# Row maxima folded into PSUM and the last stage's mask made by ScalarE, in a fused attention and mixture-of-experts kernel

## The chip, the cores and the metric

The kernel runs on one core of one Trainium2 chip. The metric is the device time of one execution in microseconds, the median of several runs. Engines are named as in the profile: PE is TensorE (PEld its weight loads), DVE is VectorE, ACT is ScalarE, POOL is GpSimd, SP issues DMAs.

## What is computed

Three parts in a row, all in float32, on 2 batches, 8 heads, 768 tokens and a head size of 64:

```python
# 1. attention within hash buckets
mask = q_bucket[:, :, :, None] == k_bucket[:, :, None, :]
scores = np.where(mask, scale * q @ k.T, -1e9)
scores = scores - scores.max(-1, keepdims=True)
attn = np.exp(scores); attn = attn / (attn.sum(-1, keepdims=True) + 1e-9)
x = (attn @ v) laid out as [1536, 512]
# 2. noisy top-2 gate over 8 experts, each relu(x @ w1[e]) @ w2[e], mixed by its weight
# 3. last layer
h = x @ w_in            # 512 -> 2048
g = h - np.tanh(h)
out = g @ w_out         # 2048 -> 512
```

A bucket is the pattern of signs of six projections of a query or key.

## The kernel before, in words

**Attention.** The 16 heads (2 batches of 8) run through a plan of frames that is written out by hand: `plan` maps a frame number to tasks, `frame` first advances the generators that are still running and then starts the frame's tasks, and the order in which instructions are emitted is the order in which each engine runs them (a manual schedule for PE, DVE, ACT and SP). A head takes 12 frames. In each frame `smax` (L410) multiplies one of six chunks of 128 queries with half of the keys into a PSUM bank of list "b", and DVE reduces the 384 columns to a maximum (L417) into a tile `mx` of [128, 6 chunks, 2 halves]. In frame 12 of the head `mchain` (L419) folds the two halves to the row maximum, twice: once rounded into the float32r tile `n2` and once exact into `m` (L424, a scalar_tensor_tensor with the constant NEGB as a third term); L425 writes the rounding's remainder behind it in `n2`, and L428 marks rows without any key in their bucket. A frame later `mrows` (L431) transposes `n2` on PE (L434), and one frame on DVE multiplies the result with a block mask into the rows of `QC` that subtract the maximum (L438). From frame 15 on `st_unit` (L442) makes the transposed scores (L448, L449) and ACT their exponential (L450); `pv` (L474) multiplies with the values, `psum` (L483) adds the exponentials up, mostly on POOL, and `evac` (L514) turns the head's output back with transposes (L523).

**PSUM.** There are eight banks in lists: "a" has banks 0, 1 and 7, "b" 2 and 3, "c" 4 and 5, "d" 6. `bank(tag)` takes the next of a list in turn; who takes a bank waits until the last user of that bank is done. List "a" serves the transposes of q and k (`turn`), their sign products, `mrows`, `vmean`, the sums, `evac` and the gate's transposes.

**Experts.** Segments of rows per expert, each in steps of a hidden block of 128: `h_mm` (12 matmuls, L1035 to L1037: every product of float32 is made of three float32r products, high×high, high×low, low×high), Relu on ACT, the remainder on DVE (L1061), and `y_mm` (L1067 to L1069).

**The last layer.** 4 blocks of 384 tokens times 16 hidden blocks are 64 steps. `h2_step` (L1336) multiplies into a bank of list "b" and emits for the step: the square s of h (ACT, L1343, `g_s`), the square of s plus a constant (L1346, `g_u`), a copy of h (L1347, `g_h`), its tanh (L1348), h − tanh(h) on POOL (L1350, `g_th`), and a polynomial in s for small |h|, three scalar_tensor_tensor on DVE (`poly`, L1354, L1356, L1358), the last of them multiplying with h. POOL's comparison of s with the constant GS makes a uint8 mask `g_m` (L1349), by which DVE's copy_predicated puts h − tanh(h) over the polynomial where |h| is large (L1368). That copy belongs to the step before (`prev`) and is emitted ahead of the polynomial of the step itself (`cur`); ACT rounds its result to float32r `hh` (L1369) and DVE takes the remainder `hl` (L1374). `o2_step` (L1384) then multiplies with w_out into three banks, two steps behind `h2_step` (LA = 2). `later` holds DVE work on the next block's tokens and on the last weights, of which `flush` emits one piece before and one piece behind `hl`. The last weights' first halves are copied by ACT (L815), their remainders come by `later` (L806).

Of the kernel before, what the change touches and what calls it, by code (L numbers as in the profile page):

```python
# [6 lines left out]
F32 = mybir.dt.float32  # L7
# [4 lines left out]
U32 = mybir.dt.uint32  # L12
U8 = mybir.dt.uint8
AF = mybir.ActivationFunctionType
ALU = mybir.AluOpType
AX = mybir.AxisListType
# [46 lines left out]
NEGB = -8.0e9  # L63
BIG = 1.0e6

G0, G1, G2, G3 = 0.33333329336821954, -0.13332532264343036, 0.05371515194576347, -0.019268172807345496
GS = 0.16
# [13 lines left out]
def body(tc, q, k, v, proj, w_gate, w_noise, noise, w1, w2, w_in, w_out, out):  # L81
    nc = tc.nc
    PS = bass.MemoryType.PSUM
    B, H, S, D = q.shape
    NC = S // 128
    NP = H // 2
    HF = S // 2
# [16 lines left out]
    with ExitStack() as ctx:  # L104
        pool = lambda name, bufs, **kw: ctx.enter_context(tc.tile_pool(name=name, bufs=bufs, **kw))
        const = pool("const", 1)
# [9 lines left out]
        def bank(tag):  # L116
            r = banks[tag]
            nbank[tag] += 1
            n = r[nbank[tag] % len(r)]
            return psp.tile([128, 512], F32, tag=f"b{n}", name=f"bank{n}")  # L120
# [10 lines left out]
        wk = att2.enter_context(tc.tile_pool(name="wk", bufs=2, side="right"))  # L131
# [86 lines left out]
        for st in range(3):  # L218
            for par in range(0 if st < 2 else 1, 2):
                i = (st, par)  # L220
# [7 lines left out]
            if st == 0:  # L228
                mask = kqp[1].tile([128, NC, 128], F32, name="mask")

        pj = const.tile([128, 64], F32, name="pj")
        nc.vector.memset(pj, 0.0)
        for o_, sg in ((0, 1.0), (NB6, -1.0), (32, -1.0), (32 + NB6, 1.0)):
# [29 lines left out]
        hd = {}  # L263
# [145 lines left out]

        def smax(i, c, hf):  # L410
            g, par = divmod(i, 2)
            if (c, hf) == (0, 0):
                hd["mx", i] = wk.tile([128, NC, 2], F32, name="mx")
            ps = bank("c" if i == 0 and hf else "b")
            r = rows_x(par)
            nc.tensor.matmul(ps[:, :HF], QC[sn(g, par)][r, ck(c)], KB[sn(g, par)][r, half(hf)], start=True, stop=True)  # L416
            nc.vector.tensor_reduce(hd["mx", i][:, c, hf:hf + 1], ps[:, :HF], op=ALU.max, axis=AX.X)  # L417

        def mchain(i):  # L419
            mx_ = hd["mx", i]  # L420
            n2 = wk.tile([128, 2 * NC], F32R, name="n2")
            m = wk.tile([128, NC], F32, name="m")
            for o_ in (n2[:, 0:NC], m):
                nc.vector.scalar_tensor_tensor(o_, mx_[:, :, 0], NEGB, mx_[:, :, 1], op0=ALU.max, op1=ALU.max)  # L424
            nc.vector.tensor_tensor(n2[:, NC:2 * NC], m, n2[:, 0:NC].bitcast(F32), op=ALU.subtract)  # L425
            hd["n2", i] = n2
            nm = wk.tile([128, NC], F32, name="nm", bufs=3)
            nc.vector.tensor_scalar(nm, m, NEGB, None, op0=ALU.is_le)  # L428
            hd["nm", i] = nm

        def mrows(i):  # L431
            g, par = divmod(i, 2)
            ps = bank("a" if i else "c")
            nc.tensor.matmul(ps[0:2 * NC, 0:128], hd["n2", i], identr, start=True, stop=True)  # L434
            yield
            n_ = NC if i else NC // 2
            for c in range(0, NC, n_):
                nc.vector.tensor_tensor(QC[sn(g, par)][mrow(par)].rearrange("p (c t) -> p c t", c=NC)[:, c:c + n_],  # L438
                                        ps[0:2 * NC, None, 0:128].to_broadcast([2 * NC, n_, 128]),
                                        mask[0:2 * NC, c:c + n_], op=ALU.mult)  # L440
# [591 lines left out]
        def h_mm(ps, t, xh, xl, n):  # L1032
            ws = lambda part, dc: t[:, part, 0, ck(dc)]
            for dc in range(KD4):
                nc.tensor.matmul(ps[:, :n], ws(0, dc), xh[:, dc, :n], start=(dc == 0), stop=False)  # L1035
                nc.tensor.matmul(ps[:, :n], ws(0, dc), xl[:, dc, :n], start=False, stop=False)  # L1036
                nc.tensor.matmul(ps[:, :n], ws(1, dc), xh[:, dc, :n], start=False, stop=(dc == KD4 - 1))  # L1037
# [107 lines left out]
        mm, mx = {}, {}  # L1145
# [146 lines left out]
        TB = 384  # L1292
# [38 lines left out]
        def flush(n):  # L1331
            for fn in later[:n]:
                fn()
            del later[:n]

        def h2_step(cur, prev):  # L1336

            tl = lambda name, dt=F32: m2.tile([128, TB], dt, name=name)
            if cur is not None:
                ps = bank("b")  # L1340
                h_mm(ps, WT["m", cur[1]], XH2[cur[0]], XL2[cur[0]], TB)
                s_, hs, th, u, big = tl("g_s"), tl("g_h"), tl("g_th"), tl("g_u"), tl("g_m", U8)
                nc.scalar.activation(s_, ps[:, :TB], AF.Square)  # L1343

            def begin():
                nc.scalar.activation(u, s_, AF.Square, bias=gb2)  # L1346
                nc.scalar.activation(hs, ps[:, :TB], AF.Copy)  # L1347
                nc.scalar.activation(th, hs, AF.Tanh)  # L1348
                nc.gpsimd.tensor_scalar(big, s_, GS, None, op0=ALU.is_gt)  # L1349
                nc.gpsimd.tensor_tensor(th, hs, th, op=ALU.subtract)  # L1350

            def poly(k):
                if k == 0:
                    nc.vector.scalar_tensor_tensor(u, u, G1 / G3 - (G2 / (2 * G3)) ** 2, s_, op0=ALU.add, op1=ALU.mult)  # L1354
                elif k == 1:
                    nc.vector.scalar_tensor_tensor(u, u, G0 / G3, s_, op0=ALU.add, op1=ALU.mult)  # L1356
                else:
                    nc.vector.scalar_tensor_tensor(u, u, G3, hs, op0=ALU.mult, op1=ALU.mult)  # L1358

            end = cur is not None and cur == steps2[-1]  # L1360
            if end:
                begin()
                poly(0)
            if prev is not None:
                hh = hp.tile([128, TB], F32R, name="hh")
                hl = hp.tile([128, TB], F32R, name="hl")
                u_, big_, th_ = GG[prev]
                nc.vector.copy_predicated(u_, big_, th_)  # L1368
                nc.scalar.activation(hh, u_, AF.Copy)  # L1369
                if end:  # L1370
                    poly(1)
                    poly(2)
                flush(1)
                nc.vector.tensor_tensor(hl, u_, hh.bitcast(F32), op=ALU.subtract)  # L1374
                flush(1)
                GG[prev] = (hh, hl)
            if cur is not None:
                if not end:
                    begin()
                    for k in range(3):  # L1380
                        poly(k)
                GG[cur] = (u, big, th)
# [24 lines left out]
        for n in range(1, NSG):  # L1407
# [8 lines left out]
            if last:  # L1416
                store()
                m2 = ctx.enter_context(tc.tile_pool(name="m2", bufs=2, side="right", reuse_waits="tile"))
                gb2 = m2.tile([128, 1], F32, name="gb2")
                nc.vector.memset(gb2, G2 / (2 * G3))  # L1420
            fx = 2 if n == B - 1 else 1
            for f in seg_steps(n, None if last else n + 1):
                if (n, f) == (1, IFS):
# [31 lines left out]
        for n in range(-LA, len(steps2)):  # L1455
# [4 lines left out]
            blk, f = at(n + LA) or (NBK, 0)  # L1460
# [42 lines left out]
```

## Time and profile before

| what | value |
|---|---|
| median of 3 runs | 980.91 us (980.35 to 982.03) |
| profiled execution, its own time | 981.7 us |
| span of its trace | 979.9 us |
| PE busy | 921.3 us (94%) |
| DVE busy | 741.0 us (76%) |
| ACT busy | 516.5 us (53%) |
| POOL busy | 455.0 us (46%) |
| granted PE clock, mean | 0.98 of full speed |

Matmuls overlap in the engine, and the ends of their rows are modelled, so PE's own pace is read from start to start. In a row of a group the numbers behind the bar are the group's busy time in us and the mean of one instruction in ns. "idle" is the time that the engine stood still just before such an instruction, with what ended it.

### The profile page before, as it was taken

What the parts mean: (1) busy time and instruction counts of PE and PEld (TensorE: products, weight loads), DVE (VectorE), ACT (ScalarE), POOL (GpSimd) and SP (SyncE); (2) the same over time, 40 slices, a digit from 0 to 9 for tenths busy, and PEclk for the clock granted to TensorE, in tenths of its full rate; (3) what the DMA queues carried; (4) which work ended last, traced back from release to release, by engine and by line L of the source; (5) the groups of instructions that cost most, each with busy time, mean ns of one, the idle gap of its engine ahead of it and who ended that gap; (6) DMA issues with size and microseconds to landing.
All of it is one profiled execution on the core that took longest, in us unless ns stands there. A gap on an engine that the chain in (4) does not pass through costs nothing.

```text
span 979.9 us, 13966 instructions
## 1 busy us (share of the span) xinstructions
PE 921.3 (94%) x4736; PEld 687.9 (70%) x4736; DVE 741.0 (76%) x1277; ACT 516.5 (53%) x1071; POOL 455.0 (46%) x388
## 2 busy tenths in 40 slices
PE   8989989978999988999999999999999999999996
PEld 3545555544545877777878877888778878888885
DVE  8788787898565518778786866546988888888885
ACT  7657666745445234545444544445655655655654
POOL 6686668756656444000000005503665665665553
PEclk9899999999899898999999999999999999999998
DMA  5644453313201587785867768355300210210000
GB/s 129 163 119 141 151 188 94 85 29 127 71 1 43 169 253 235 228 274 188 274 216 246 251 212 271 128 162 176 108 23 1 66 31 1 67 31 1 33 1 32
DMA packets 104244, 122.96 MB, mean 125 GB/s; under 512 B 32121, under 2 KB 75177, under 8 KB 104169
## 3 DMA queue, kind: packets, MB, share of 16 engines
q1 hardware_dynamic: 100328, 109.44, 36.1%
q0 software_dynamic: 3840, 12.59, 3.9%
q8 instruction: 38, 0.62, 0.3%
q14 instruction: 38, 0.30, 0.1%
HBM read 82.00 MB, written 37.72 MB: 122 GB/s over the span
## 4 chain that ended last, share of the span: by engine, by line
PE 53%; DVE 34%; issue 4%; ACT 3%; DMA 3%; POOL 2%; DVEq 0%; SPq 0%; POOLq 0%; ACTq 0%
DVE g_u L1358 8%; PE bank L474 6%; PE bank L1035 5%; PE bank L1036 5%; PE bank L1037 5%; PE bank L1069 4%; DVE g_u L1356 4%; PE bank L1068 4%; PE bank L1067 4%; PE bank L448 4%; DVE g_u L1354 4%; DVE hl L1374 4%; DVE g_u L1368 3%; PE bank L449 3%; PE bank L416 3%
## 5 line engine op out<-in xcount | busy, mean ns | idle before, releaser
L1035 PE MATMUL bank<-xh,wt 128*128 128x384 f32 (+2 forms) x544 | 187.5, 345 | 3.1 <-ACT xh L1029 2.0
L1036 PE MATMUL bank<-xl,wt 128*128 128x384 f32 (+2 forms) x544 | 183.7, 338 | 1.1 <-DVE xl L1030 1.1
L1037 PE MATMUL bank<-xh,wt 128*128 128x384 f32 (+2 forms) x544 | 183.5, 337 | 0.0
L1067 PE MATMUL bank<-wt,hh 128*128 128x512 f32 (+1 forms) x400 | 161.9, 405 | 12.6 <-ACT hh L1369 8.5
L1069 PE MATMUL bank<-wt,hl 128*128 128x512 f32 (+1 forms) x400 | 161.2, 403 | 1.4 <-DVE hl L1374 1.0
L1068 PE MATMUL bank<-wt,hh 128*128 128x512 f32 (+1 forms) x400 | 158.6, 397 | 0.0
L806 POOL TENSOR_TENSOR wt<-wraw,wt 128x512 fp32r<-128x512 f32 x32 | 46.4, 1472 | 231.1 <-PE bank L1037 213.4
L417 DVE TENSOR_REDUCE mx<-bank 128x1 f32<-128x384 f32 x192 | 103.2, 552 | 40.9 <-PE bank L416 39.2
L450 ACT ACTIVATE p<-bank 128x384 f32<-128x384 f32 x192 | 91.9, 489 | 71.2 <-PE bank L449 68.4
L1035 PEld LDWEIGHTS bank<-xh,wt 128*128 128x128 f32 x544 | 102.6, 189 | 16.9 <-PE bank L1084 4.9
L1350 POOL TENSOR_TENSOR g_th<-g_h,g_th 128x384 f32<-128x384 f32 x64 | 65.3, 1021 | 105.7 <-ACT g_th L1348 105.7
L1036 PEld LDWEIGHTS bank<-xl,wt 128*128 128x128 f32 x544 | 102.8, 189 | 7.8 <-DVE xl L1030 1.3
L1037 PEld LDWEIGHTS bank<-xh,wt 128*128 128x128 f32 x544 | 102.7, 189 | 3.1
L1349 POOL TENSOR_SCALAR g_m<-g_s 128x384 uint8<-128x384 f32 x64 | 91.9, 1436 | 16.4 <-ACT g_s L1343 16.2
L1067 PEld LDWEIGHTS bank<-wt,hh 128*128 128x128 f32 (+1 forms) x400 | 75.6, 189 | 30.1 <-ACT hh L1369 13.0
L1369 ACT ACTIVATE hh<-g_u 128x384 fp32r<-128x384 f32 x64 | 33.6, 525 | 118.6 <-DVE g_u L1368 118.6
L1069 PEld LDWEIGHTS bank<-wt,hl 128*128 128x128 f32 (+1 forms) x400 | 75.5, 189 | 26.7 <-DVE hl L1374 9.3
L483 POOL TENSOR_TENSOR ps<-ps,p 128x768 f32<-128x768 f32 x46 | 84.0, 1825 | 11.8 <-ACT p L450 7.1
L474 PE MATMUL bank<-p,v 128*64 128x384 f32 x384 | 85.0, 522 | 0.0
L1068 PEld LDWEIGHTS bank<-wt,hh 128*128 128x128 f32 (+1 forms) x400 | 75.8, 189 | 12.5
L448 PE MATMUL bank<-qc,kb 108*128 108x384 f32 (+1 forms) x192 | 81.7, 426 | 1.9 <-DVE qc L438 1.6
L1052 ACT ACTIVATE hh<-bank 128x384 fp32r<-128x384 f32 (+1 forms) x80 | 35.4, 443 | 86.7 <-PE bank L1037 67.3
(255 smaller groups left out, 1782.1 us busy)
## 6 DMA issues: line engine op xcount, KB each, us to landing
wraw<-in_moe_w_dram SPq DMA_DIRECT2D x80, 256.0 KB
w2r<-in_moe_w_dram SPq DMA_DIRECT2D x48, 256.0 KB
cv_t<-in_moe_w_in_dram SPq DMA_DIRECT2D x16, 512.0 KB
cv_t<-in_moe_w_out_dram SPq DMA_DIRECT2D x16, 512.0 KB
W2f<-cv_w SPq DMA_DIRECT2D x16, 512.0 KB
wraw<-W2f SPq DMA_DIRECT2D x16, 512.0 KB
Xg<-zero SPq DMA_DIRECT2D x14, 512.0 KB
Y<-zero SPq DMA_DIRECT2D x9, 512.0 KB
```

The lines of the kernel that those rows point to most:

```text
L417: nc.vector.tensor_reduce(hd["mx", i][:, c, hf:hf + 1], ps[:, :HF], op=ALU.max, axis=AX.X)
L448: nc.tensor.matmul(ps[:, :HF], KB[sn(g, par)][r, ck(kc)], QC[sn(g, par)][r, half(hf)], start=True, stop=False)
L450: nc.scalar.activation(hd["p", i, kc][:, half(hf)], ps[:, :HF], AF.Exp, scale=float(D) ** -0.5)
L474: nc.tensor.matmul(hd["o", i][hf * D:(hf + 1) * D, :HF], raw["v", g][:, par, kc], hd["p", i, kc][:, half(hf)], start=(kc == 0), stop=(kc = ...
L483: eng.tensor_tensor(t, hd["p", i, 0] if kc == 1 else t, hd["p", i, kc], op=ALU.add)
L1035: nc.tensor.matmul(ps[:, :n], ws(0, dc), xh[:, dc, :n], start=(dc == 0), stop=False)
L1036: nc.tensor.matmul(ps[:, :n], ws(0, dc), xl[:, dc, :n], start=False, stop=False)
L1037: nc.tensor.matmul(ps[:, :n], ws(1, dc), xh[:, dc, :n], start=False, stop=(dc == KD4 - 1))
L1067: nc.tensor.matmul(ps[:m], a, t[:, 0, 1], start=first, stop=False)
L1068: nc.tensor.matmul(ps[:m], a, t[:, 1, 1], start=False, stop=False)
L1069: nc.tensor.matmul(ps[:m], l, t[:, 0, 1], start=False, stop=last)
L1349: nc.gpsimd.tensor_scalar(big, s_, GS, None, op0=ALU.is_gt)
```

## The change

`mchain` now works on two fixed tiles `MX`, used by even and odd heads, with a third column that holds NEGB. The maximum over the three columns is a tensor_reduce, and the exact result `m` goes into columns 256 to 261 of the PSUM bank that `mrows` used to take a frame later and that it now shares. In the last layer the mask is ACT's Relu of s − GS, a float32 that is above zero where s is above GS and whose bits copy_predicated reads as uint32; the comparison on POOL is gone. The polynomial's last step reads h from PSUM in place of the copy `hs`.

```diff
+        MX = [const.tile([128, NC, 3], F32, name=f"mx{j}") for j in range(2)]
+        for t in MX:
+            nc.vector.memset(t[:, :, 2:3], NEGB)
...
         def smax(i, c, hf):
             g, par = divmod(i, 2)
-            if (c, hf) == (0, 0):
-                hd["mx", i] = wk.tile([128, NC, 2], F32, name="mx")
...
-            nc.vector.tensor_reduce(hd["mx", i][:, c, hf:hf + 1], ps[:, :HF], op=ALU.max, axis=AX.X)
+            nc.vector.tensor_reduce(MX[i % 2][:, c, hf:hf + 1], ps[:, :HF], op=ALU.max, axis=AX.X)
 
         def mchain(i):
-            mx_ = hd["mx", i]
+            mx_ = MX[i % 2]
+            ps = hd["mps", i] = bank("a" if i else "c")
             n2 = wk.tile([128, 2 * NC], F32R, name="n2")
-            m = wk.tile([128, NC], F32, name="m")
+            m = ps[:, 256:256 + NC]
             for o_ in (n2[:, 0:NC], m):
-                nc.vector.scalar_tensor_tensor(o_, mx_[:, :, 0], NEGB, mx_[:, :, 1], op0=ALU.max, op1=ALU.max)
+                nc.vector.tensor_reduce(o_, mx_, op=ALU.max, axis=AX.X)
             nc.vector.tensor_tensor(n2[:, NC:2 * NC], m, n2[:, 0:NC].bitcast(F32), op=ALU.subtract)
...
         def mrows(i):
             g, par = divmod(i, 2)
-            ps = bank("a" if i else "c")
+            ps = hd["mps", i]
...
-                s_, hs, th, u, big = tl("g_s"), tl("g_h"), tl("g_th"), tl("g_u"), tl("g_m", U8)
+                s_, hs, th, u, big = tl("g_s"), tl("g_h"), tl("g_th"), tl("g_u"), tl("g_m")
...
             def begin():
...
                 nc.scalar.activation(th, hs, AF.Tanh)
-                nc.gpsimd.tensor_scalar(big, s_, GS, None, op0=ALU.is_gt)
                 nc.gpsimd.tensor_tensor(th, hs, th, op=ALU.subtract)
+                nc.scalar.activation(big, s_, AF.Relu, bias=gsb)
...
                 else:
-                    nc.vector.scalar_tensor_tensor(u, u, G3, hs, op0=ALU.mult, op1=ALU.mult)
+                    nc.vector.scalar_tensor_tensor(u, u, G3, ps[:, :TB], op0=ALU.mult, op1=ALU.mult)
...
-                nc.vector.copy_predicated(u_, big_, th_)
+                nc.vector.copy_predicated(u_, big_.bitcast(U32), th_)
...
                 gb2 = m2.tile([128, 1], F32, name="gb2")
                 nc.vector.memset(gb2, G2 / (2 * G3))
+                gsb = m2.tile([128, 1], F32, name="gsb")
+                nc.vector.memset(gsb, -GS)
```

## Rows read from the trace of the kernel before

**Rows 1.** Last stage: us, then busy PE, PEld, DVE, ACT, POOL; clock, DMA

```profile
676.00:976.00 300.00, 283.25 (x1381) 243.24 (x1379) 253.08 (x351) 171.29 (x357) 174.88 (x146) 0.99 0.12 36
```

**Rows 2.** PE in order of time, last stage: start us, us, engine, line, operation

```profile
675.96 0.33 PE L1035 MATMUL bank<-xh,wt 128*128 128x384 f32 x1
...
895.92 0.33 PE L1035 MATMUL bank<-xh,wt 128*128 128x384 f32 x1
...
898.02 0.39 PE L1067 MATMUL bank<-wt,hh 128*128 128x512 f32 x1
...
900.11 0.33 PE L1035 MATMUL bank<-xh,wt 128*128 128x384 f32 x1
...
975.11 0.39 PE L1069 MATMUL bank<-wt,hl 128*128 128x512 f32 x1
```

**Rows 3.** Groups by line, shapes apart

```profile
L1325 PE MATMUL bank<-ident,xy 128*128 128x128 f32 x48 | 7.4, 276 | 1.8 <-DVE xl L1328 1.8
...
L1061 DVE SCALAR_TENSOR_TENSOR hl<-bank,hh 128x384 fp32r<-128x384 f32 x48 | 26.5, 553 | 12.3 <-ACT hr L1060 12.3
...
L1346 ACT ACTIVATE g_u<-g_s,gb 128x384 f32<-128x384 f32 x64 | 38.5, 602 | 0.1
```

**Rows 4.** ACT and POOL in order of time, one step of the last stage

```profile
896.99 0.53 ACT L1369 ACTIVATE hh<-g_u 128x384 fp32r<-128x384 f32 x1 [2.05 <-DVE g_u L1368]
...
898.42 0.53 ACT L1348 ACTIVATE g_th<-g_h 128x384 f32<-128x384 f32 x1
...
899.10 1.01 POOL L1350 TENSOR_TENSOR g_th<-g_h,g_th 128x384 f32<-128x384 f32 x1 [1.94 <-ACT g_th L1348]
900.08 1.47 POOL L1349 TENSOR_SCALAR g_m<-g_s 128x384 uint8<-128x384 f32 x1
...
901.37 0.53 ACT L1369 ACTIVATE hh<-g_u 128x384 fp32r<-128x384 f32 x1 [2.04 <-DVE g_u L1368]
```

**Rows 5.** DVE in order of time, the same step

```profile
898.65 0.56 DVE L1356 SCALAR_TENSOR_TENSOR g_u<-g_u,g_s 128x384 f32<-128x384 f32 x1
899.31 1.21 DVE L1358 SCALAR_TENSOR_TENSOR g_u<-g_u,g_h 128x384 f32<-128x384 f32 x1
900.62 0.71 DVE L1368 COPY_PREDICATED g_u<-g_m,g_th 128x384 f32<-128x384 uint8 x1
```

**Rows 6.** Line 425 (ns least/median/most), and head 3 in order of time

```profile
L425 DVE TENSOR_TENSOR n<-m,n x16: 165/329/1786, 20.6 to 285.4; 128x6 fp32r<-128x6 f32 x16
...
67.64 5.63 POOL L483 TENSOR_TENSOR ps<-ps,p 128x768 f32<-128x768 f32 x3
...
71.51 1.79 DVE L425 TENSOR_TENSOR n<-m,n 128x6 fp32r<-128x6 f32 x1
```

**Rows 7.** What PE waited for, attention stage, 20 to 310 us: total, times, longest

```profile
PE bank L434 <- DVE nm L428: 10.5, 9, 1.5
...
PE bank L434 <- DVE n L425: 3.2, 2, 1.6
```

**Rows 8.** Lines 285 and 1368: ns least/median/most, first and last start

```profile
L285 DVE TENSOR_TENSOR ql<-bank,qc x28: 539/552/560, 7.7 to 238.3; 64x384 fp32r<-64x384 f32 x28
...
L1368 DVE COPY_PREDICATED g_u<-g_m,g_th x64: 575/711/847, 682.1 to 969.8; 128x384 f32<-128x384 uint8 x64
```

**Rows 9.** PE and DVE in order of time, around the mrows matmul of head 6

```profile
124.39 0.23 PE L434 MATMUL bank<-ident,n 128*12 128x128 f32 x1 [1.48 <-DVE nm L428]
124.45 0.50 PE L523 MATMUL bank<-ident,ot 128*128 128x128 f32 x3
...
125.41 0.95 DVE L438 TENSOR_TENSOR qc<-bank,mask 12x768 fp32r<-12x768 f32 x1
```

**Rows 10.** DVE and ACT in order of time, a step with weights

```profile
693.81 1.33 DVE L1356 SCALAR_TENSOR_TENSOR g_u<-g_u,g_s 128x384 f32<-128x384 f32 x1
...
691.59 0.53 ACT L1369 ACTIVATE hh<-g_u 128x384 fp32r<-128x384 f32 x1 [1.10 <-DVE g_u L1368]
...
696.54 0.52 ACT L1369 ACTIVATE hh<-g_u 128x384 fp32r<-128x384 f32 x1 [1.66 <-DVE g_u L1368]
```

## The prediction

> **What bounds the kernel now.** I read the busy time by stage first, then the order of time on each engine inside one step of the last stage, then PE's waits in the attention stage.
>
> The last stage (h = x·w_in, g = h − tanh(h), g·w_out) takes the stretch from 676 to 976 us. PE is called busy for 283 of its 300 us [rows 1], but a busy PE is not a PE at its pace. Its own pace shows in one step [rows 2]: the twelve matmuls of the first product start at 895.92, the nine of the second at 898.02, the next twelve at 900.11, so 2.10 + 2.09 = 4.19 us. 64 steps are 268 us, and the 36 transposes of that stage at most 7.4 × 36/48 = 5.5 us [rows 3], 273.5 together. From the first matmul to the end of the last one 975.50 − 675.96 = 299.5 us pass [rows 2]. So about 26 us of that stage are PE waiting, and this is the most that a faster DVE can give there.
>
> What PE waits for is a loop over ACT, DVE and POOL. ACT starts hh at 896.99 and the next hh at 901.37: 4.38 us per step [rows 4], longer than PE's 4.19. In it DVE runs hl and the three polynomial steps, and the third (L1358, two operands in SBUF) takes 1.21 us from 899.31, although the second (L1356, same form) took 0.56 [rows 5]. At 899.31 POOL is inside its subtraction (899.10 to 900.11) [rows 4]; L1358 ends 0.41 us after POOL does. Then copy_predicated starts (900.62, 0.71 us) and releases hh.
>
> The same pattern sits in the attention stage: DVE's L425, on six columns, takes 0.165 us at best and 1.786 at worst, and at 71.51 it ends as POOL's additions end (67.64 + 5.63 = 73.27) [rows 6]. PE waits for that short chain with its mrows matmul (L434): 10.5 + 3.2 = 13.7 us over the heads [rows 7]. Operations that take one operand from PSUM are not held: L285 lies between 539 and 560 ns in all 28 cases, in the stage where POOL is busiest [rows 8].
>
> **The change part by part.**
>
> *mchain.* Two two-operand instructions become reductions with one SBUF operand; the subtraction and the comparison read m from PSUM. No instruction of the chain has two SBUF operands any more. The reductions' price has no row at this size; the nearest are 0.165 us (L425's least) [rows 6] and 0.55 us, L285's whole 384 columns, as the upper bound [rows 8]. I take 0.165, since 18 elements are nearer to six than to 384: four instructions, 0.66 us. At the head of [rows 6] the new chain would be through at about 72, where the old L425 ended at 73.3. PE came to its wait there 1.3 us before the end (13.7 us over 11 waits [rows 7] are 1.25 each), so nearly all of those waits go. I keep 0.5 us for the heads where the chain was short already: 13.2 us.
>
> What it adds: m's bank is taken one frame earlier and is held until mrows' product (L438) has read it. Bank list "a" has three banks, so the third allocation behind it must wait for L438. Counting the allocations of a pair of heads by frame, for heads 6 and 10 the third is evac's transposes, which today stand directly behind L434 on PE (124.45), while L438 runs from 125.41 for 0.95 us [rows 9]. With DVE's 1.7 us stall gone L438 comes earlier; I put 1.2 us on each of the two, between 0 and 1.9 (126.36 − 124.45) each. Behind that wait on PE stand the scores of the running head, and ACT's exponentials wait for those. For heads 4, 8 and 12 it is the transposes of q, a frame later than L438: nothing, covered by the score and pv matmuls between; 1 us each without them. The two memsets of MX, the one of gsb and the wider g_m tile go at nothing: DVE's start and the stage's start cover them, and bare they are three instructions of 0.165 us. Sum 13.2 − 2.4 = 10.8; as another wait may come next in the same head (the next head's row maxima against DVE) I count 9, with 4 and 13 as ends.
>
> *L1358 from PSUM.* It loses its second SBUF operand. The nearest row is L1061, the same operation from PSUM and SBUF with the same shape: 553 ns [rows 3]. So 1.21 becomes 0.55. Bank b is freed by it and no longer by hs, about 0.9 us later in the step; PE needs that bank two steps on, so nothing waits, and without that cover it would be those 0.9 us.
>
> [...]
>
> *The mask.* POOL loses 64 comparisons of 1.47 us [rows 4]; no DMA is added or moved, and the gathers, which stand behind the comparison in POOL's queue, come earlier. ACT gets one more pass, of the form of L1346 (SBUF, bias from a tile): 602 ns [rows 3]. In a step ACT waits 2.04 us for copy_predicated before hh [rows 4], so it lies beside other work; uncovered it would be 0.6 × 64 = 38 us. It stands behind tanh and is done before POOL's subtraction of 1.01 us, so copy_predicated doesn't wait for it. Behind it on ACT stand the next square, the weights' first half and, at a block's end, the evacuations, all of them in the time in which ACT waits for copy_predicated today.
>
> [...]
>
> copy_predicated then reads a four-byte mask in place of a one-byte one. Its own row gives 575 ns at least, 711 at the median and 847 at most [rows 8]; the least is from the stage's end, where POOL's comparison is not in its way. I take 0.58, with 0.85 as the upper end.
>
> *The new step.* From hh's start to the end of POOL's subtraction 900.11 − 896.99 = 3.12 us [rows 4]. The handover from POOL to DVE has no row; from ACT to POOL it is 0.15 (tanh ends at 898.95, the subtraction starts at 899.10) [rows 4], I take 0.1, ends 0.03 and 0.2. Then 0.58 and 0.04 to ACT (901.33 to 901.37) [rows 4, 5]: 3.84, ends 3.75 and 4.2. DVE's own way through hl and the polynomial ends with L1358 at about 899.31 + 0.55 = 899.86, ahead of the subtraction. So the loop falls below PE's 4.19, and PE becomes the bound of the plain steps.
>
> What is late next: five steps at the stage's start carry the halves of the last weights. There the second polynomial step already meets POOL's subtraction (L1356 at 693.81, 1.33 us) and the step from hh to hh is 696.54 − 691.59 = 4.95 us [rows 10]; the change doesn't touch that. I leave 5 × (4.95 − 4.19) = 3.8, rounded to 5 as two of these steps also have a gather on POOL; 3 for the three block boundaries, where PE waits for banks that ACT evacuates, and for the fill. 26 − 8 = 18 us gained, ends 8 and 25.
>
> Sum: 9 + 18 = 27. The profiled execution took 981.7 us (span 979.9 and 1.8 around it), 0.8 above the median of the runs: 981.7 − 27 = 954.7, or **954** beside the median of 980.9. About 0.2%, 2 us, is what a measurement of this kernel can tell from no change.
>
> **The rivals.**
>
> 1. *The wait moves from L1358 to copy_predicated.* If the handover and the wider mask cost their upper ends, the step is 4.2 to 4.25 and not 3.84. For it: the margin is 0.35 us and two of its terms have no row. Against: copy_predicated took 575 ns where POOL's comparison was away [rows 8]. The stage then gains some 56 × 0.15 = 8 us and the attention 9: 964.
>
> 2. *The attention gives nothing*, because the waits for m's bank take what the shorter chain gives: 2 × 1.9 + 3 × 1 us and an equal amount in later row maxima. For it: three banks serve all of these tasks. Against: only heads 4, 6, 8, 10 and 12 are touched, the waits [rows 7] lie mostly elsewhere. 981.7 − 18 = 963.
>
> 3. *Slower: the four-byte mask doubles copy_predicated and more.* It stands in the loop in each of the 64 steps. It decides from the point where the loop is above 4.38, that is copy_predicated above 0.58 + 0.54 = 1.12 us, and turns the whole slower from 1.26 us on, where 64 × 0.14 eats the 9 us of the attention. At 1.47 us, what POOL takes for its pass over the mask [rows 4], the step is 4.73: 64 × 0.35 − 9 = 13 us slower, 994. Against: it would be the only DVE pass over 384 columns at over 1 us without POOL in its way.
>
> 4. *The change doesn't do what it says*: L1358 is slow for its place in the order and not for its second SBUF operand. Against: at 693.81 us it is L1356 that is held, in the heads L425 [rows 6, 10], and PSUM operands never [rows 8]. Then only the comparison leaves POOL: within 2 us of 981.
>
> 5. *Nearly all of PE's waits go*, 25 + 13 us: 943.
>
> **How the numbers follow.** The forecast of 954 has 0.58, rival 1 0.20, rival 2 0.10, rival 3 0.04, rival 4 0.03, rival 5 0.05. Rivals 1, 2 and 5 are faster too: faster 0.93, the same 0.03, slower 0.04. The forecast's own ends are 946 (13 + 22 us) and 963 (4 + 14); to hold eight in ten the range goes to rivals 1, 2 and 5: 943 to 967, a few us above 964 for both shortfalls in part.
>
> **What would show it.** Right: L1358 at about 0.55 us in all 64 cases; no comparison on POOL; hh to hh at PE's 4.19 in the plain steps with DVE idle before copy_predicated, released by POOL's subtraction; mchain's four instructions all below 0.25 us, and L434's waits near zero; evac's transposes waiting for L438 at heads 6 and 10. Wrong: steps still at 4.38, copy_predicated above 0.85 us, ACT's mask releasing it, or the time saved before 300 us given back before 676.

## The result and the profile after

The changed kernel takes 946.1 us (median of 4 runs, 945.6 to 948.2) beside 980.7 us for the kernel before on the same chip: a ratio of 0.9649, 95% interval 0.9631 to 0.9666, so about 34.6 us less. Its profiled execution has a span of 943.8 us, 36.1 less than 979.9. One run of an experiment below, the row maxima alone, fell into a slower state (1108.0 us, granted clock 0.75) and is left out of its median.

The span splits at the first matmul of the last stage. It starts at 662.81 us instead of 675.96 [rows 2], 13.15 us earlier, and the stage from there to the end of the last matmul takes 939.41 − 662.81 = 276.6 us instead of 299.5, 22.9 less. Nothing that the first part gains is given back between the two. Of the 13.15 us, 10.4 are won when the last head's mrows matmul starts (PE, the kernel before and then the changed one); the experiments below show that the other 2.8 are not the change's.

```profile
287.18 0.23 PE L434 MATMUL bank<-ident,n 128*12 128x128 f32 x1 [1.60 <-DVE n L425]
...
276.79 0.22 PE L438 MATMUL bank<-ident,n 128*12 128x128 f32 x1
```

In the new kernel the lines of the last stage have moved down by four: h_mm's matmuls are L1039 to L1041, the polynomial L1358, L1360 and L1362, copy_predicated L1372, hh L1373, hl L1378. The mrows matmul is L438, its product L442, evac's transposes L527.

The window of the last stage (us, then busy PE, PEld, DVE, ACT, POOL with instruction counts; clock, DMA share, GB/s) answers to [rows 1]:

```profile
663.00:940.00 277.00, 273.54 (x1380) 245.55 (x1379) 201.27 (x350) 202.78 (x421) 88.97 (x82) 1.00 0.12 38
```

POOL has lost half its work (174.9 us before, with the comparisons), ACT has gained about 31, and PE is called busy for all but 3.5 us.

One plain step, first ACT, then POOL, then DVE in order of time [rows 4, 5]:

```profile
883.01 0.52 ACT L1373 ACTIVATE hh<-g_u 128x384 fp32r<-128x384 f32 x1
...
884.45 0.53 ACT L1352 ACTIVATE g_th<-g_h 128x384 f32<-128x384 f32 x1
884.88 0.60 ACT L1354 ACTIVATE g_m<-g_s,gsb 128x384 f32<-128x384 f32 x1
886.81 0.49 ACT L1347 ACTIVATE g_s<-bank 128x384 f32<-128x384 f32 x1 [1.34 <-PE bank L1041]
887.20 0.52 ACT L1373 ACTIVATE hh<-g_u 128x384 fp32r<-128x384 f32 x1
...
885.05 1.05 POOL L1353 TENSOR_TENSOR g_th<-g_h,g_th 128x384 f32<-128x384 f32 x1 [3.13 <-ACT g_th L1352]
...
885.32 0.55 DVE L1362 SCALAR_TENSOR_TENSOR g_u<-g_u,bank 128x384 f32<-128x384 f32 x1
886.13 0.60 DVE L1372 COPY_PREDICATED g_u<-g_m,g_th 128x384 f32<-128x384 uint32 x1 [0.25 <-POOL g_th L1353]
```

hh to hh is now 4.19 us, PE's own step, where it was 4.38. L1362 runs inside POOL's subtraction (885.05 to 886.10) and takes 0.55 us; L1358 of before took 1.21 in the same place. copy_predicated begins 0.03 us after the subtraction and is through at 886.73, but ACT starts hh only at 887.20: it waits first for PE (the square, 886.81) and does hh after it. In this step ACT's wait is on PE, no longer on DVE.

The touched lines over the whole kernel (ns least/median/most, first and last start) [rows 6, 8]:

```profile
L428 DVE TENSOR_REDUCE n<-mx x16: 158/162/173, 20.5 to 275.9; 128x6 fp32r<-128x18 f32 x16
L428 DVE TENSOR_REDUCE bank<-mx x16: 168/169/170, 20.6 to 276.0; 128x6 f32<-128x18 f32 x16
...
L429 DVE TENSOR_TENSOR n<-bank,n x16: 162/164/165, 20.8 to 276.2; 128x6 fp32r<-128x6 f32 x16
...
L432 DVE TENSOR_SCALAR nm<-bank x16: 152/154/157, 20.9 to 276.3; 128x6 f32<-128x6 f32 x16
...
L1362 DVE SCALAR_TENSOR_TENSOR g_u<-g_u,bank x64: 553/554/556, 667.6 to 934.2; 128x384 f32<-128x384 f32 x64
...
L1372 DVE COPY_PREDICATED g_u<-g_m,g_th x64: 581/599/614, 668.4 to 935.4; 128x384 f32<-128x384 uint32 x64
```

No instance of the chain or of L1362 is held any more: the longest of each row is within 15 ns of its shortest.

What PE waited for (total us, times, longest), the attention stage first [rows 7], then all that is left in the last stage, and last the two largest waits of that stage in the kernel before:

```profile
PE bank L527 <- DVE qc L442: 3.1, 2, 1.6
...
PE bank L438 <- DVE nm L432: 0.4, 1, 0.4
...
PE bank L1039 <- DVE g_u L1362: 2.7, 5, 1.0
...
PE bank L1067 <- ACT hh L1369: 8.5, 10, 1.9
PE bank L1067 <- ACT wraw L1393: 3.9, 3, 2.2
```

13.7 us of PE waits for the short chain have become 0.4; 3.1 us are new, for the bank that now holds m. In the last stage a wait for bank b is all that remains; the waits for hh and, at the block boundaries, for the banks that ACT evacuates (wraw) are gone.

### The profile page after: what moved, and what is told of

Read it like the earlier page. It is cut to its first block, busy times and chain, and to the rows that moved or that the text cites. A ratio compares the mean times of both kernels' runs of the same rounds, so it can differ in the third digit from the quotient of the medians.

```text
span 943.8 us, 13840 instructions
## 1 busy us (share of the span) xinstructions
PE 909.8 (96%) x4736; PEld 689.3 (73%) x4736; DVE 674.9 (72%) x1280; ACT 547.7 (58%) x1135; POOL 367.9 (39%) x324
## 4 chain that ended last, share of the span: by engine, by line
PE 80%; DVE 9%; DMA 4%; issue 2%; POOL 2%; ACT 1%; SPq 1%; DVEq 0%; POOLq 0%; ACTq 0%
PE bank L1039 9%; PE bank L1041 9%; PE bank L1040 9%; PE bank L1073 9%; PE bank L1072 8%; PE bank L1071 8%; PE bank L478 7%; PE bank L452 4%; PE bank L453 3%; PE bank L418 3%; PE bank L1088 2%; DMA Xg<-x,sidx 2%; PE bank L1032 1%; DVE mx L419 1%; PE bank L306 1%
## 5 line engine op out<-in xcount | busy, mean ns | idle before, releaser
L1039 PE MATMUL bank<-xh,wt 128*128 128x384 f32 (+2 forms) x544 | 187.7, 345 | 3.2 <-DVE g_u L1362 2.7
L1041 PE MATMUL bank<-xh,wt 128*128 128x384 f32 (+2 forms) x544 | 183.4, 337 | 0.0
L1071 PE MATMUL bank<-wt,hh 128*128 128x512 f32 (+1 forms) x400 | 158.4, 396 | 0.4 <-DVE wraw L1104 0.4
L1073 PE MATMUL bank<-wt,hl 128*128 128x512 f32 (+1 forms) x400 | 158.1, 395 | 0.4 <-DVE hl L1065 0.2
L1072 PE MATMUL bank<-wt,hh 128*128 128x512 f32 (+1 forms) x400 | 157.9, 395 | 0.0
L1039 PEld LDWEIGHTS bank<-xh,wt 128*128 128x128 f32 x544 | 102.8, 189 | 18.4 <-PE bank L1088 4.9
L1041 PEld LDWEIGHTS bank<-xh,wt 128*128 128x128 f32 x544 | 102.9, 189 | 2.9
L452 PEld LDWEIGHTS bank<-qc,kb 108*128 108x128 f32 (+1 forms) x192 | 37.0, 193 | 50.8 <-ACT p L454 32.2
L418 PE MATMUL bank<-kb,qc 96*128 96x384 f32 (+1 forms) x192 | 67.4, 355 | 4.8 <-DVE mx L419 3.8
```

The lines of the kernel that those rows point to most:

```text
L452: nc.tensor.matmul(ps[:, :HF], KB[sn(g, par)][r, ck(kc)], QC[sn(g, par)][r, half(hf)], start=True, stop=False)
L1071: nc.tensor.matmul(ps[:m], a, t[:, 0, 1], start=first, stop=False)
L1072: nc.tensor.matmul(ps[:m], a, t[:, 1, 1], start=False, stop=False)
L1073: nc.tensor.matmul(ps[:m], l, t[:, 0, 1], start=False, stop=last)
```

## The experiments

The kernel before took 980.7, 981.4, 991.3 and 981.6 us in the four sets of runs, which were not all on one chip, so runs are compared by their ratio to the kernel before on the same chip, and by lengths inside the trace.

**Half and half.** The first kernel has only the mchain part of the change, the second only the last stage's two parts.

> Only the attention part of the change; the last stage is as before. My theory (the short chain after the row maxima was held by POOL's additions because its instructions read two operands in SBUF, and now reads none so): the time before 663 us of the changed kernel comes alone, 13 us below before, 966 to 969 us, with the last stage still 299 us long. Rival (the two parts work only together, the attention's gain being given back later by the unchanged last stage): at most 5 us, 976 or more.

> Only the last stage's part; the attention is as before. My theory: the last stage falls from 299.5 to about 276.5 us as in the changed kernel, in all 956 to 960 us. Rival (the last stage gains from an earlier or calmer start): less than 18 us, 963 or more.

Measured on one chip (before 981.4 us): the row maxima alone 970.7 us, ratio 0.9905 (0.987 to 0.9941); the last stage alone 956.9 us, ratio 0.9756 (0.973 to 0.9782). The first lies just above its bracket, the second inside its own. The traces show where the time goes (us; the clock is the granted one between the two starts):

```
                          last head's mrows   last stage starts   between   clock   last stage takes
before                    287.18              675.96              388.8     0.98    299.5
row maxima alone          276.90              663.01              386.1     0.99    300.2
last stage alone          287.75              673.89              386.1     0.99    276.4
mask alone (below)        286.64              675.73              389.1     0.98    285.8
changed kernel            276.79              662.81              386.0     0.98    276.6
```

The attention part gives 10.4 us in the pair of the result and 10.9 on this chip (287.75 against 276.90). What lies between takes 386.1 with the new attention and 386.1 with the old one, so the 2.8 us by which the kernel before was longer there belong to its execution and not to the change; why executions differ there was not tried. So each part gives its gain in its own stage, some 10.5 and 23 us, and they add.

**The last stage's two parts one by one.** First the polynomial's operand alone, then the mask alone:

```diff
-                    nc.vector.scalar_tensor_tensor(u, u, G3, hs, op0=ALU.mult, op1=ALU.mult)
+                    nc.vector.scalar_tensor_tensor(u, u, G3, ps[:, :TB], op0=ALU.mult, op1=ALU.mult)
```

> Only one operand is changed: the third polynomial step reads h from PSUM; POOL still makes the mask by its comparison. My theory (that step waited for POOL's subtraction because both its operands lay in SBUF): it takes 0.55 us in place of 1.2, the loop from hh to hh falls below PE's 4.19 us, and nearly all of the last stage's gain comes, 18 to 22 us, 959 to 963. Rival (POOL's comparison, 1.47 us per step, is what holds the loop): the loop stays near 4.38 and the time within 4 us of before.

```diff
-                nc.gpsimd.tensor_scalar(big, s_, GS, None, op0=ALU.is_gt)
                 nc.gpsimd.tensor_tensor(th, hs, th, op=ALU.subtract)
+                nc.scalar.activation(big, s_, AF.Relu, bias=gsb)
...
-                nc.vector.copy_predicated(u_, big_, th_)
+                nc.vector.copy_predicated(u_, big_.bitcast(U32), th_)
```

> Only the mask moves to ACT; the third polynomial step still reads the copy of h in SBUF. My theory: that step still waits for POOL's subtraction (about 1.2 us), copy_predicated falls from 0.71 to 0.60, the loop to about 4.27 us, still above PE's 4.19: 4 to 10 us gained, 971 to 977. Rival (the comparison's leaving POOL is the gain): the stage falls by 18 us or more, 963 or less.

Measured (same chip): operand alone 965.7 us, ratio 0.9832 (0.9802 to 0.9863); mask alone 968.0 us, ratio 0.9869 (0.9841 to 0.9897). Both missed their bracket, the operand giving 2.7 us less and the mask 3.0 us more than the nearer end. In the traces the last stage takes 281.3 and 285.8 us, so 18.3 and 13.8 us less than before; the two sum to 32, more than the 26 us that PE stood in all (299.5 − 273.5), and both together give 23. The distances from hh to hh show what each does, 63 in each kernel, read from ACT in order of time:

```
last stage          median step   steps over 4.6 us, and their sum beyond 4.19   stage
before              4.39          16      16.5 us                                299.5 us
operand alone       4.13          14      16.5 us                                281.3 us
mask alone          4.28          10       7.2 us                                285.8 us
both (changed)      4.19          11       7.2 us                                276.6 us
```

There are two losses. One is the plain step of 4.39 instead of 4.19, some 8.5 us over the other steps, the very last aside. The operand mends it and more: freed of the hold, steps run at 3.8 to 4.1 us where PE's products already lie there (3.79 from hh at 735.94 to 739.73). The mask alone leaves the hold and takes only 0.11 off:

```profile
883.05 1.19 DVE L1358 SCALAR_TENSOR_TENSOR g_u<-g_u,g_h 128x384 f32<-128x384 f32 x1
884.37 0.60 DVE L1368 COPY_PREDICATED g_u<-g_m,g_th 128x384 f32<-128x384 uint32 x1
...
880.73 0.52 ACT L1369 ACTIVATE hh<-g_u 128x384 fp32r<-128x384 f32 x1 [0.75 <-DVE g_u L1368]
...
885.00 0.53 ACT L1369 ACTIVATE hh<-g_u 128x384 fp32r<-128x384 f32 x1 [0.84 <-DVE g_u L1368]
```

L1358 is still held (1.19 us), and copy_predicated goes from 0.71 to 0.60 since no comparison runs beside it: a step of 4.27.

The other loss is the long steps, and most of these I had not looked at. In the kernel before, POOL and then ACT in order of time in one of them:

```profile
770.82 1.20 POOL L1305 DMA_INDIRECT xy<-Y,yidx  x1 [0.15 <-issue]
772.32 0.95 POOL L1305 DMA_INDIRECT xy<-Y,yidx  x1 [0.30 <-issue]
773.30 1.44 POOL L1349 TENSOR_SCALAR g_m<-g_s 128x384 uint8<-128x384 f32 x1
774.73 1.01 POOL L1350 TENSOR_TENSOR g_th<-g_h,g_th 128x384 f32<-128x384 f32 x1
...
771.82 0.53 ACT L1369 ACTIVATE hh<-g_u 128x384 fp32r<-128x384 f32 x1 [1.90 <-DVE g_u L1368]
...
777.10 0.52 ACT L1369 ACTIVATE hh<-g_u 128x384 fp32r<-128x384 f32 x1 [2.94 <-DVE g_u L1368]
```

Two gathers hold POOL until 773.27; then the comparison, 1.44 us, still stands ahead of the subtraction that the loop waits for. tanh is through at about 773.8 (1.96 us after hh starts, as in [rows 4]), the subtraction begins 0.95 later, and the step takes 5.28 us instead of about 4.3. Without the comparison the gathers are absorbed: with the mask alone six of the 16 long steps and 9.3 us of the excess are gone, with the operand alone two steps and none of the excess. That is the larger part of the mask's worth, and it lies on POOL's queue, not on DVE.

Why the two don't add shows in what PE waited for hh, 8.5 us before: with the operand alone and with the mask alone.

```profile
PE bank L1067 <- ACT hh L1369: 0.3, 2, 0.2
...
PE bank L1067 <- ACT hh L1369: 4.3, 7, 1.7
```

With the operand alone the gather steps are as long as before, but the short steps give the loop a lead: hh of 772.90 is done at 773.42, and PE starts on it only at 776.46. The long steps that follow (5.38, 5.60 and 5.62 us) eat this lead of 3.0 us instead of stopping PE; before, hh of 777.10 was done at 777.62 and PE took it 0.06 us later. So either cure also pays for part of the other's loss.

**The mask's price on ACT.** The changed kernel with the Relu pass written twice:

> The changed kernel with the mask's pass on ACT run twice into the same tile, 64 times 0.5 to 0.6 us more on ACT. My theory (ACT has 1.33 us of idle time in a plain step, and the loop 0.4 us of slack beside PE): the plain steps stay at 4.19 us, the steps with weights lose a little, 946 to 950 in all. Rival (ACT is now close to being the bound): 0.3 us or more on each step, 965 or more.

Measured on another chip (before 991.3 us): 959.2 us, ratio 0.9676 (0.9643 to 0.971), whose interval holds the changed kernel's 0.9649. Its last stage takes 278.9 us, 2.3 more than the changed kernel's, for 64 more passes of 617 ns, 39.5 us of ACT. copy_predicated now waits for the second pass and no longer for POOL:

```profile
DVE hl L1379 <- ACT hh L1374: 40.5, 52, 1.6
DVE g_u L1373 <- ACT g_m L1355: 17.9, 53, 0.3
```

ACT's slack takes the pass, as forecast: of its idle time before the square, 1.34 us in the step shown above, 0.68 is left beside a second one (before 887.71 us). The plain step is still 4.19 us with it, and the stage begins to lengthen.

**Which half of mchain frees it.** First the reductions with m in SBUF (the old way of allotting the bank), then m in PSUM with the two-operand instructions kept:

```diff
-                nc.vector.scalar_tensor_tensor(o_, mx_[:, :, 0], NEGB, mx_[:, :, 1], op0=ALU.max, op1=ALU.max)
+                nc.vector.tensor_reduce(o_, mx_, op=ALU.max, axis=AX.X)
```

> The kernel before with only the reductions over three columns; m stays in SBUF and the bank is taken a frame later as before. My theory: the reductions take 0.17 us always, but the subtraction behind them still reads two operands in SBUF and the comparison still reads SBUF, so one of these is held until POOL's current addition ends; PE's waits for the chain stay at 10 us or more, the time within 4 us of before, 977 to 982. Rival (what counts is that the maximum over three columns is a cheaper instruction): most of the attention's 13 us, 966 to 971.

```diff
-            m = wk.tile([128, NC], F32, name="m")
+            ps = hd["mps", i] = bank("a" if i else "c")
+            m = ps[:, 256:256 + NC]
```

> The kernel before with only m in PSUM; the maximum is still the instruction with two operands in SBUF, run twice. My theory: the first of the two is held by POOL's addition in place of a later one, so PE's waits stay at 8 us or more and the time within 5 us of before, 976 to 982. Rival (reading m from PSUM is what counts): most of the attention's 13 us, 966 to 971.

Measured (the chip with 991.3 us): the reductions alone 979.8 us, ratio 0.9884 (0.9844 to 0.9925); m in PSUM alone 985.8 us, ratio 0.9941 (0.9919 to 0.9962). The first was expected to give at most 4 us and gave 11.5, as much as the whole part; my theory, that a hold only moves on to the next two-operand instruction, fell. The second gave 5.5 where at most 5 were expected, and PE's waits for the chain fell to 4.7 us where 8 or more were. The chain in the kernel with the reductions alone (lines as above, m in SBUF), then the same head as in [rows 6], on DVE and POOL, and the chain's first instruction there in the kernel before:

```profile
L425 DVE TENSOR_REDUCE m<-mx x16: 159/161/165, 19.8 to 278.4; 128x6 f32<-128x18 f32 x16
L426 DVE TENSOR_TENSOR n<-m,n x16: 165/214/1555, 20.0 to 278.6; 128x6 fp32r<-128x6 f32 x16
...
L429 DVE TENSOR_SCALAR nm<-m x16: 157/162/1808, 20.2 to 278.9; 128x6 f32<-128x6 f32 x16
...
71.09 0.17 DVE L426 TENSOR_TENSOR n<-m,n 128x6 fp32r<-128x6 f32 x1
71.17 0.17 DVE L429 TENSOR_SCALAR nm<-m 128x6 f32<-128x6 f32 x1
67.38 5.67 POOL L484 TENSOR_TENSOR ps<-ps,p 128x768 f32<-128x768 f32 x3
...
71.08 0.32 DVE L424 SCALAR_TENSOR_TENSOR n<-mx 128x6 fp32r<-128x6 f32 x1
```

The subtraction is still held sometimes (1.56 us at most), but here it passes between two of POOL's additions (67.38 + 2 × 1.89 = 71.16) at no cost. Before, the first two-operand instruction waited for that boundary (71.08, 0.32 us), the second passed right behind it, and the subtraction, begun 0.1 us past it, waited for the next one (1.79 us [rows 6]). So in this chain two instructions were held, each by another of POOL's additions, by 0.16 and 1.63 us over the 0.16 of an instance that is not held, and what sent the chain past the boundary was the hold before. The chain's first instruction comes some 0.3 us ahead of that boundary in either kernel, so part of the reductions' gain hangs on where these heads' chains happen to begin. Adding up all instances of the chain over 0.25 us, less 0.16 each, beside PE's waits for it:

```
                          held instances   held us   PE waits for the chain   PE waits for m's bank (L527's kind)
before                    26               22.9      13.7 us                  none
reductions, m in SBUF     11                9.3       4.3                     none
two-operand, m in PSUM    14               10.1       4.7                     3.4
both, without the rest     0                0         0.5                     3.1
changed kernel             0                0         0.4                     3.1
```

PE's waits fit the times: 13.7 − 4.3 = 9.4 us less for the reductions, 13.7 − 4.7 − 3.4 = 5.6 for m in PSUM. Either half takes away over half of the held time; m in PSUM then pays 3 us for its bank, so the second half of the change is worth next to nothing by this table. That was tried by itself next.

**Four kernels on one chip** (before 981.6 us). The changed kernel again, as base; bank b with a third bank; the mrows block one slot earlier; and the changed kernel with m back in SBUF:

> The changed kernel unaltered, timed on the chip of the three that follow, as their base. Both theories: its ratio to the kernel before is the measured 0.965 within its interval (0.963 to 0.967); a PE wait of about 3 us in attention for m's bank (evacuation transposes, 2 times) and one of about 3 us in the last stage for bank b (5 times) are in its trace again.

```diff
         store()
+        banks.update(a=[0], b=[2, 3, 1])
         hd["second"] = True
```

> The changed kernel with the last stage's banks dealt out anew: bank group b, which the polynomial's last step now holds until it has run, gets a third bank, taken from group a. Theory: the 2.7 us that PE waits there in the last stage (5 times, all in the steps that convert weights) disappear, and the time falls by 0 to 3 us against the changed kernel on this chip. Rival: group a, left with one bank, makes PE wait for the transposes' copies instead, and the time stays or rises by 1 to 5 us.

```diff
-mrows=(13, 13)
+mrows=(12, 13)
```

> The changed kernel with the transposition of the row-maxima block put one slot earlier in the plan (12 in place of 13), so that the bank that now holds m is free earlier. Theory: the evacuation's 3.1 us of PE wait for that bank (2 times, 1.6 at the longest) shrink or go, and the time falls by 1 to 3 us. Rival: PE reaches the transposition before VectorE has finished the chain and waits there instead, so that the waits for the chain grow from 0.4 us and the time is the same or up to 3 us longer.

```diff
-            ps = hd["mps", i] = bank("a" if i else "c")
...
-            m = ps[:, 256:256 + NC]
+            m = wk.tile([128, NC], F32, name="m")
...
-            ps = hd["mps", i]
+            ps = bank("a" if i else "c")
```

> The changed kernel with m back in SBUF: the fold over three columns stays, the PSUM target goes. The earlier pair of runs says that the reductions take away the first of two holds in a chain and that m in PSUM takes away the second (held time in all chains: 22.9 us before, 9.3 with the reductions alone, none with both), and that m in PSUM has a price of its own, the evacuation's wait of 3.1 us for its bank. Theory: PE waits for the chain rise from 0.4 to about 4 us, the 3.1 us go, and the time is within 2 us of the changed kernel. Rival (the PSUM target is what makes the fold worth having): 4 us or more slower than the changed kernel.

```
                              median     ratio to before (95%)        last stage starts at, takes
changed kernel again          946.4 us   0.9652 (0.9625 to 0.9679)    663.6, 276.6 us
third bank for b              956.9      0.9749 (0.9721 to 0.9777)    664.5, 287.1
mrows one slot earlier        950.3      0.9695 (0.9669 to 0.9720)    666.1, 276.6
m back in SBUF                945.4      0.9644 (0.9617 to 0.9671)    662.2, 276.6
```

The third bank removes bank b's wait and costs 10.5 us: group a, left with one, makes PE stand at each block boundary. PE's waits in its last stage, and the first of them in order of time:

```profile
PE bank L1329 <- DVE xl L1332: 7.5, 3, 3.0
PE bank L1071 <- ACT hh L1373: 1.5, 5, 0.3
...
719.86 1.09 PE L1329 MATMUL bank<-ident,xy 128*128 128x128 f32 x4 [2.98 <-DVE xl L1332]
```

The rival was right, at twice its price. The waits, 9.0 us less the 2.7 that are gone, are not all of the 10.5: the granted clock was 0.83 from 715 to 725 us and 0.86 from 858 to 870, around the first and the third of these waits, where it was 1.00 over the changed kernel's whole stage; whether that makes up the rest is not shown. The earlier mrows block also went the rival's way, 3.9 us slower, a little beyond its end. The bank's wait is gone, and PE now arrives before the chain is done:

```profile
PE bank L438 <- DVE nm L432: 6.4, 7, 2.0
PE bank L418 <- DVE mx L419: 5.2, 5, 1.9
```

With m back in SBUF the time is 1.0 us below the base, which the intervals don't tell from none. Its trace has both sides of the trade, the chain held 10.8 us in 11 instances, and PE waiting for the chain 4.4 + 1.3 us while the 3.1 us for m's bank are gone:

```profile
PE bank L437 <- DVE nm L431: 4.4, 5, 1.9
...
PE bank L437 <- DVE n L428: 1.3, 1, 1.3
```

So m in PSUM is worth nothing measurable on top of the reductions. That kernel is the simpler one at equal speed, and none was found that beats the changed one by more than the measurement tells.

## Why the prediction was right, and where it was off

The forecast was 954 and the time is 946: the mechanism held in the main, and the gain was 34.6 us instead of 27. It lies at the forecast's own lower end (946), nearest to rival 5 (nearly all PE waits go, 943).

**mchain.** That the chain is no longer held once none of its instructions has two SBUF operands was right: no instance over 0.173 us, by 0.162 and 0.169 for the reductions where 0.165 was taken. L434's waits went from 13.7 to 0.4, as counted (13.2). The new wait of evac's transposes for m's bank came at heads 6 and 10, as counted from the allocation order, at 1.57 us each instead of 1.2. PE and then DVE in order of time at head 6:

```profile
117.88 0.22 PE L438 MATMUL bank<-ident,n 128*12 128x128 f32 x1
119.67 0.55 PE L527 MATMUL bank<-ident,ot 128*128 128x128 f32 x3 [1.57 <-DVE qc L442]
...
118.66 0.95 DVE L442 TENSOR_TENSOR qc<-bank,mask 12x768 fp32r<-12x768 f32 x1
```

The step that failed is the last one, "I count 9": 1.8 us were taken off 10.8 for a wait that might come next in the same head, and none came. The mrows matmul of the last head starts at 276.79 instead of 287.18 us, 10.4 earlier (10.9 in the experiments), where the sum had 10.8. The other 2.8 us up to the last stage are not the change's, as the two halves show. One thing the forecast took for granted was not needed: it paid 2.4 us for m's bank, and the reductions with m left in SBUF give the same time.

**L1358 from PSUM.** 554 ns at the median in 64 instances, for 0.55 forecast. The two steps ahead of it, the same operation with both operands in SBUF, take 559 and 558 ns at the median (L1358 and L1360 of the changed kernel), so reading h from PSUM shows no price of its own. "PE needs that bank two steps on, so nothing waits" was wrong at the stage's start and in the steps that carry weights. There L1360 is held by the subtraction, L1362 comes late, and PE stands for bank b (DVE, then PE):

```profile
683.72 1.26 DVE L1360 SCALAR_TENSOR_TENSOR g_u<-g_u,g_s 128x384 f32<-128x384 f32 x1
685.08 0.55 DVE L1362 SCALAR_TENSOR_TENSOR g_u<-g_u,bank 128x384 f32<-128x384 f32 x1
...
685.69 0.44 PE L1039 MATMUL bank<-xh,wt 128*128 128x384 f32 x1 [0.41 <-DVE g_u L1362]
```

Bank b is free only when L1362 has run (685.63). That costs 2.7 us in five instances, four of 0.41 to 0.45 in the weight steps and one of 0.99 at the stage's start (668.25); the experiment that gave bank b a third bank only moved the stall.

**The mask and the step.** ACT's pass took 602 ns as forecast and lay beside other work. copy_predicated took 0.60 and not 0.58 (its least before, 575 ns at 966.96, was not a free place as the forecast had it: the comparison on POOL ran from 965.82 to 967.29), the handover from POOL 0.03 and not 0.1; the loop, where nothing else held it, ran at 3.75 us (steps at the stage's start), forecast 3.84. That is below PE's 4.19 with 0.4 to spare, so rival 1 (a margin eaten up) fell, and rival 3 too: the four-byte mask cost nothing that shows (600 ns at the median with either width, as the last section has it). With ACT idle in a plain step (1.34 us above) and the loop running through DVE, the pass on ACT shows only as one wait of DVE of 0.5 us (L1362 for L1354), and a second pass cost the stage 2.3 us. A mask made by DVE was not tried.

**What was left of PE's stall.** This is the term that was mis-sized: 8 us were left (5 in the weight steps, 3 at block boundaries and for the fill), and 3.1 are (276.6 less the 273.5 of PE's own work, in which the transposes stand at their most). Of the 3 us for block boundaries and fill, PE's wait of 0.99 at the start is left; its waits at the boundaries (3.9 us for the evacuations) and for hh (8.5) are gone altogether. Of the 5 in the weight steps, PE's four waits of 0.41 to 0.45 are left. These steps stay at 4.90 us from hh to hh (forecast 4.95), but "the change doesn't touch that" was wrong for the two of them with gathers, which fell from 5.94 to 4.91 as the comparison left POOL. The six gather steps further on (5.26 to 5.53 us) the forecast had not seen. It counted what they cost as gained, without a reason; it is gained because the comparison is no longer queued behind the gathers and because a loop below PE's step builds a lead, and the forecast had worked out neither, so this part is luck (the operand alone leaves 7.8 us, 281.3 − 273.5). In numbers: 26 − 8 = 18 forecast, 26 − 3.1 = 22.9 measured.

Of the rivals, 2 (the attention gives nothing) and 4 (the operand isn't the cause) fell: 10.4 us earlier at the end of the attention, and 1.21 became 0.55 with nothing but the operand changed.

## What to carry to other kernels

When a DVE instruction shows a longest time near the duration of a POOL instruction (here 1.79 us beside 1.88 for one of POOL's additions [rows 6]), count the DVE instructions in a row that read two SBUF operands: at head 3 two of them were held (0.32 and 1.79 us), and here folding the first ones into a one-operand form gave all of the measurable gain (945.4 us without m in PSUM, 946.4 with it). Before a stall is split into plain steps times an excess, list the distances between steps: a few long ones can hold the larger part, with a cause of their own (here 16 of 63 held 16.5 us, of which 9.3 went with a POOL pass queued between gathers and the work that the loop waits for). Two cures of one loop didn't add here (18.3 and 13.8 us alone, 22.9 together), as one alone already brought its short steps below the next bound (3.79 beside PE's 4.19 us): the faster loop gains a lead, 3.0 us here, that also covers its long steps. And the bank that one of them holds longer has a price at another place (2.7 us of PE's waits for bank b).

## What the hardware showed that I had not expected

The hold is not tied to an operation but to when it is issued: the same subtraction took 1.79 us in the kernel before, where it began 0.1 us into one of POOL's additions [rows 6], and 0.17 at the same head with the reductions alone, where it came at the boundary of two of them (1.56 at most over the heads). The 16 + 16 reductions from SBUF in that kernel took 0.174 us at most. Beside another instruction of POOL's, a memset, the subtraction was not held in the kernel before (0.17 us), and the comparison behind it was, to the memset's end (0.60).

```profile
20.55 0.73 POOL L408 MEMSET qc<- 12x768 f32 x1
...
20.62 0.17 DVE L425 TENSOR_TENSOR n<-m,n 128x6 fp32r<-128x6 f32 x1
20.71 0.60 DVE L428 TENSOR_SCALAR nm<-m 128x6 f32<-128x6 f32 x1
```

To have only one operand in SBUF was not enough to be safe: with the reductions alone L429, the comparison with a constant whose operand and result both lie in SBUF, took 0.162 us at the median and 1.808 at most; with m in PSUM it took 0.157 at most (L432 of the changed kernel).

copy_predicated, which has two inputs in SBUF, is held less than the polynomial (1.21 us for L1358 [rows 5]): 0.71 us at the median where POOL's comparison follows the subtraction, 0.60 in the changed kernel, and at most 0.92 in the one with the operand alone, where 24 of its 64 instances fall wholly into a comparison and end 0.20 to 0.22 us ahead of it. The width of the mask makes no difference (600 ns at the median with one byte, operand alone, and 600 with four, mask alone). Why it isn't held to the end of POOL's instruction was not tried.
